# One head ahead of the others: reordering the start of a clustered-attention kernel, and moving copies from VectorE to ScalarE

## The chip, the core and the metric

The kernel runs on one core of a Trainium2 chip. Its time is the device time of one execution in microseconds (us); the time before is the median of three runs. Engines are called as the profile calls them: PE is TensorE's matmul side (PEld its weight loads), DVE VectorE, ACT ScalarE, POOL GpSimd, SP SyncE.

## The reference

Attention over 4 batches, 8 heads, 768 tokens and a head size of 64, in which a query sees a key only if both fall into the same of 16 clusters; then a gated feed-forward layer (512 to 1536 to 512) on its output.

```python
q_assign = np.argmax(np.einsum('bhsd,hcd->bhsc', q_n, c_n), axis=-1)
k_assign = np.argmax(np.einsum('bhsd,hcd->bhsc', k_n, c_n), axis=-1)
mask = q_assign[:, :, :, None] == k_assign[:, :, None, :]
scores = np.where(mask, scale * np.matmul(q, k.transpose(0, 1, 3, 2)), -1e9)
attn = softmax(scores)                       # written out in the reference
x = np.matmul(attn, v)                       # heads side by side: 3072 x 512
xn = x / np.sqrt(np.mean(x * x, -1, keepdims=True) + 1e-06) * rms_g
g = xn @ w_gate
out = (g * sigmoid(g) * (xn @ w_val)) @ w_out
```

## The kernel before

**The mask as extra rows.** The kernel never builds the mask. For each head it keeps q and k transposed in bf16, `qext` and `kext`, 64 rows each, and below them 16 rows with a one in the row of the token's cluster. The score product over 80 rows is then the plain score plus a large constant where the clusters agree, and the exponential with a bias of minus that constant (`off`) leaves nothing of the others.

**Making the operands of a head.** `trans(g, h, part)` (L202) transposes k (part 1) or q (part 0) of head h of group g on PE in three products into a PSUM tile `tq` and copies it to `qkT` in SBUF, on ACT (L214) or, if told so, on DVE (L212). A group is four heads: half a batch. `cast` (L220) writes the bf16 rows from `qkT`; K0, K1, Q0, Q1 in the code are the halves of k and q of a head (even and odd tokens in the first four groups' arrays). Unit 0 needs K0, K1 and Q0 of a head before its scores, Q1 only in unit 1. For batch 0 the cluster rows come from `pair_clusters(p)` (L293): four products of 32 rows (two heads, q and k) into one PSUM tile, then on DVE a transpose in blocks of 32 (L245), the largest of each 16 (L250), and a compare with it (L254) into the tile `pads[p]`; `under(n, m)` (L298) transposes 32 rows of `pads` to below the rows of head n (L300), and `head(n)` does it for k and q.

**Units, gaps, hooks.** Attention is done in eight units: one batch, half of its queries, all eight heads. A unit has 24 gaps, each opened by `scores(u, h, i)` (L306): two products (L316) into one of two PSUM buffers of the pool `ps_s`, and one exponential on ACT of 128 x 768 (L320). In the second gap of a head come the products with v of the head before (`pv`, L324), after every second head the normalization on DVE (L339, L341). What else is issued in a gap of unit 0 is listed by hand in `first` (L605): a number is the gap, a function its work, and `more` (one dummy product that keeps PE busy) stands where there is none. The order of issue is the program's order: on each engine instructions run in the order of the text, and wait there for their operands.

**The prologue** (L519 to L555) makes heads 0 and 1 before the first scores, in this order: k, then q of head 0, k and q of head 1, the cluster steps of both together (`pair_clusters(0)`), the casts on POOL, then k and q of heads 2 and 3 and of head 4 (`tokens(1, 0)`), the second half of k of head 1 cast on ACT, two dummy products, and the rows of heads 0 and 1 by `under`. POOL's casts, conversions of v (`vcast`), the clearing of the other `pads` and the issue of weight loads stand in one line behind one another.

**The start of the feed-forward of unit 0** lies in unit 1. `rms(0)` (L362) computes the norm on DVE after the last `pv` of unit 0; in gap 5 of unit 1 `xtrans_all(0)` (L382) transposes the 128 x 512 blocks of x on PE into two PSUM tiles, `ps[0]` for columns c = 0 and 1 and `ps[1]` for c = 2 and 3, and copies them to `xnT`, scaled by `gcol`: c = 0 to 2 on DVE (L391), c = 3 on ACT (L393). Then each of 12 columns f has a gate product and a value product over the four c (L405). The q and k of group 3 are transposed in unit 1, the q copies by DVE, the k copies by ACT (L455).

Of the kernel before, what the change touches and what calls it, by code (L numbers as in the profile page):

```python
# [9 lines left out]
F32 = mybir.dt.float32  # L10
BF16 = mybir.dt.bfloat16
I32 = mybir.dt.int32
AX = mybir.AxisListType.X
ALU = mybir.AluOpType
# [8 lines left out]
def kernel(  # L23
# [12 lines left out]
    nc = tc.nc  # L36
    B, H, S, D = q.shape
    NC = centroids.shape[1]
    DM = moe_w_gate.shape[0]
    DF = moe_w_gate.shape[1]  # L40
    P = 128
    ST = S // P
    HT = ST // 2
    UQ = HT * P
    HG = 4
# [13 lines left out]
    pool = lambda n, b, **kw: ctx.enter_context(tc.tile_pool(name=n, bufs=b, **kw))  # L59
# [3 lines left out]
    asg = pool("asg", 1)  # L63
    ptp = pool("ptp", 3)
    xp = pool("xp", 1)
    small = pool("small", 3)
    gate = pool("gate", 3)
    outp = pool("outp", 3)
    ps_s = pool("ps_s", 2, space=PSUM)
    ps_a = pool("ps_a", 1, space=PSUM)  # L70
    ps_g = pool("ps_g", 3, space=PSUM)
# [13 lines left out]
    def load_qk(n):  # L85
        if n < B * H:
            load(n, 0)
            load(n, 1)

    def load_v(n, vq=None):  # L90
        if n >= B * H:
            return
        stagedv[n] = stage.tile([P, ST, D], F32, tag="vs", name="vs", bufs=NV)
        (vq or nc.sync).dma_start(out=stagedv[n], in_=src(v, n))
# [55 lines left out]
    for i in range(P // 32):  # L150
        r = slice(32 * i, 32 * i + 32)
# [12 lines left out]
    cblk = const.tile([P, H, 2 * NC], F32)  # L164
# [35 lines left out]
    qkT = {}  # L200

    def trans(g, h, part, on=None):  # L202
        if (g, h // 2) not in qkT:
            qkT[g, h // 2] = qk32.tile([P, 2, 2, UQ], F32, tag="qkT", name="qkT")
        qk = staged[g * HG + h]
        ps = ps_g.tile([P, UQ], F32, tag="gen", name="tq")
        for i in range(HT):
            nc.tensor.transpose(ps[:, i * P:(i + 1) * P], qk[:, part, 2 * i:2 * i + 2].rearrange("p t d -> p (t d)"),  # L208
                                ident_f)
        to, by = qkT[g, h // 2][:, h % 2, part], 1.0 / ZS if part else 1.0  # L210
        if on is nc.vector:
            nc.vector.tensor_scalar_mul(to, ps, by)  # L212
        else:
            nc.scalar.activation(to, ps, ACT.Copy, scale=by)  # L214
# [5 lines left out]
    def cast(on, g, h, part, es=(0, 1)):  # L220
        for e in es:
            to = cols((kext if part else qext)[g % 4][:D, h], g, e)
            of = qkT[g, h // 2][e * D:(e + 1) * D, h % 2, part]
            if on is nc.scalar:
                nc.scalar.copy(to, of)
            else:
                on.tensor_copy(to, of)  # L227

    def vcast(n):
        nc.gpsimd.tensor_copy(vbf[n // HG % 4][:, n % HG, :, :D], stagedv[n])  # L230


    scT = {}

    NB = UQ // 32

    def cluster_products(g, what, ps=None):

        if ps is None:
            ps = ps_g.tile([P, UQ], F32, tag="gen", name="sc")  # L240
        for i, (h, m) in enumerate(what):
            nc.tensor.matmul(ps[32 * i:32 * i + 32], lhsT=cblk[:, g * HG % H + h],  # L242
                             rhs=qkT[g, h // 2][:, h % 2, m], start=True, stop=True)
        sct = asg.tile([P, UQ], F32, tag="scT", name="scT", bufs=2)
        nc.vector.transpose(sct, ps)  # L245
        return sct.rearrange("p (b e c) -> p b e c", e=2, c=NC)

    def largest(cl):
        mx = small.tile([P, NB, 2], F32, tag="mx", name="mx")
        nc.vector.tensor_reduce(mx, cl, axis=AX, op=ALU.max)  # L250
        return mx

    def compare(to, cl, mx):
        nc.vector.tensor_tensor(to, cl, mx.unsqueeze(3).broadcast_to([P, NB, 2, NC]), op=ALU.is_equal)  # L254

    def cluster_steps(g, m):

        of = {}

        def products():  # L260
            of["cl"] = cluster_products(g, [(h, m) for h in range(HG)])

        def most():
            of["mx"] = largest(of["cl"])

        def same():
            of["ohT"] = asg.tile([P, UQ], BF16, tag="ohT", name="ohT", bufs=2)
            compare(of["ohT"].rearrange("p (b e c) -> p b e c", e=2, c=NC), of["cl"], of["mx"])

        def back():  # L270
            put[g, m] = asg.tile([P, UQ], BF16, tag="oh", name="oh", bufs=3)
            nc.vector.transpose(put[g, m], of["ohT"])  # L272

        return [products, most, same, back]
# [3 lines left out]
    def place(on, g, m):  # L278

        ext = (kext if m else qext)[g % 4]  # L280
        for h in range(HG):
# [7 lines left out]
    pads = [(xp if p == 0 else outp).tile([P, NB, 32, 2], BF16, tag="o_sb" if p else "gvT", name=f"pads{p}")  # L289
            for p in range(H // 2)]  # L290
    nc.gpsimd.memset(pads[0][:, :, NC:], 0.0)

    def pair_clusters(p, ps=None):  # L293
        g, h = divmod(2 * p, HG)
        cl = cluster_products(g, [(h, 0), (h + 1, 0), (h, 1), (h + 1, 1)], ps)
        compare(pads[p][:, :, :NC].rearrange("p b c e -> p b e c"), cl, largest(cl))

    def under(n, m):  # L298
        i = 32 * (2 * m + n % 2)
        nc.vector.transpose((kext if m else qext)[n // HG][D:D + 32, n % HG].bitcast(I32),  # L300
                            pads[n // 2][i:i + 32].rearrange("p b c e -> p (b c e)").bitcast(I32))

# [79 lines left out]
    def xtrans_all(u):  # L382

        xnT[u] = xp.tile([P, CC, UQ], BF16, tag="xnT", name="xnT")
        ps = [ps_g.tile([P, 2, UQ], BF16, tag="gen", name="tx") for _ in range(CC // 2)]
        for t in range(HT):
            for c in range(CC):
                nc.tensor.transpose(ps[c // 2][:, c % 2, t * P:(t + 1) * P], xn[u][:, t, c * P:(c + 1) * P], ident)
        for c in range(CC):
            if c < 3:  # L390
                nc.vector.tensor_scalar_mul(xnT[u][:, c], ps[c // 2][:, c % 2], gcol[:, c:c + 1])  # L391
            else:
                nc.scalar.activation(xnT[u][:, c], ps[c // 2][:, c % 2], ACT.Copy, scale=gcol[:, c:c + 1])  # L393
# [56 lines left out]
    def group_work(g):  # L450

        t, c = [], []
        for h in range(HG):
            n = g * HG + h
            t += [(0.3, lambda h=h: trans(g, h, 0, nc.vector if g == 3 else None)), (0.3, lambda h=h: trans(g, h, 1))]  # L455

            def others(n=n):
                vcast(n)
                load_qk(n + NQ)
                load_v(n + NV)  # L460

            def both(h=h, f=others):
                cast(nc.gpsimd, g, h, 0)
                f()
                cast(nc.vector, g, h, 1, (0,))
            if g == 2:
                c.append((0.0, others))
            else:
                c += [(0.0, both), (0.0, lambda h=h: cast(nc.vector, g, h, 1, (1,)))]
        a = []  # L470
        for m in range(2):
            a += [(0.0 if i else 0.7, f) for i, f in enumerate(cluster_steps(g, m))]
            if g <= 3:
                a.append((0.0, lambda m=m: place(nc.sync if g == 2 else nc.gpsimd, g, m)))
        if g > 3:
            a.append((0.0, lambda: [place(nc.gpsimd, g, m) for m in range(2)]))
        return t, c, a
# [25 lines left out]
    def out_work(u):  # L503
        return [(0.86, lambda t=t, p=p: out_mm(u, t, p)) for t in range(UNITS[u][2]) for p in range(3)]
# [6 lines left out]
    def tokens(g, h, on=None):  # L511
        trans(g, h, 1, on)
        trans(g, h, 0, on)

    def casts(on, n, *what):
        for m, e in what:
            cast(on, n // HG, n % HG, m, (e,))

    K0, K1, Q0, Q1 = (1, 0), (1, 1), (0, 0), (0, 1)  # L519
    pool_ = nc.gpsimd  # L520
    trans(0, 0, 1)
    centroids_t()
    trans(0, 0, 0)
    trans(0, 1, 1)
    trans(0, 1, 0)
    pair_clusters(0, ps_s.tile([P, UQ], F32, tag="s", name="sc"))
    casts(pool_, 0, K0, Q0, K1)
    casts(pool_, 1, K0, Q0)
    load_v(0)
    load_v(1)  # L530
    for n in (6, 7):
# [6 lines left out]
    nc.sync.dma_start(out=gcol, in_=moe_rms_g.rearrange("(c p) -> p c", p=P), allow_slow_non_contiguous=True)  # L538
    tokens(0, 2)
    casts(pool_, 2, K0, K1, Q0)  # L540
    tokens(0, 3)
    tokens(1, 0)
    casts(pool_, 3, K0, K1, Q0)
    casts(nc.scalar, 1, K1)
    busy(2)
    for n in (0, 1):
        under(n, 1)
        under(n, 0)
    casts(pool_, 0, Q1)
    casts(pool_, 1, Q1)  # L550
    vcast(0)
# [10 lines left out]
    def second_batch():  # L562
# [2 lines left out]
            load_qk(n)  # L565
        for n in range(H, H + NV):
            load_v(n)

    def head(n):
        under(n, 1)  # L570
        under(n, 0)

    def gap1():
        pair_clusters(1)
# [11 lines left out]
    def gap5():  # L586
# [11 lines left out]
        for n in (6, 7):  # L598
# [3 lines left out]

    early = [lambda h=h, m=m: trans(1, h, m) for h in (2, 3) for m in (1, 0)]
    late = [lambda h=h, m=m: trans(2, h, m, nc.vector if h < 3 else None) for h in range(HG) for m in (1, 0)]
    first = {1: gap1, 2: early[0], 3: early[1], 4: lambda: (early[2](), early[3]()), 5: gap5,  # L605
             7: lambda: head(5), 9: lambda: pair_clusters(3), 10: lambda: head(6),
             13: lambda: (casts(nc.vector, 6, K0, K1), head(7)), 14: lambda: (more(), second_batch())}
    first.update({16: None, 19: None, 22: None})
# [26 lines left out]
    for u in range(1, NU):  # L635
        ffn, o, g = ffn_work(u - 1), out_work(u - 2) if u > 1 else [], u + 2
        if u == 1:
            t, c, a = group_work(2)
            t3, c3, a3 = group_work(3)
            n = LEAD - 4  # L640
# [61 lines left out]
```

The softmax here doesn't subtract the row's maximum and nothing guards it: scores larger than these inputs give would overflow.

## Time and profile before

| | |
|---|---|
| time | 350.19 us (349.99 to 350.3) |
| profiled span | 348.0 us, granted PE clock 1.00 |
| first score product | 11.23 us |
| first exponential | 11.77 us |
| first scores of unit 1 | 33.62 us |
| last `pv` of unit 0 ends | 35.47 us |
| last norm step of x, unit 0 (L369) ends | 40.13 us |
| last of the first four gate products starts | 42.25 us |

The page gives each engine's busy time, then the span in 40 slices of 8.7 us, with the busy share of each engine in tenths. The chain of waits goes back from the last instruction to what released it, over and over; a piece of time on it belongs to the instruction that the end was then waiting for. The timeline lists instructions with start, duration, engine, line, operation, what is written from what with shapes, and in square brackets the idle time before it and who ended it. The start of PE's stretch of L316 to the start of its exponential is the time from scores to ACT.

### The profile page before, as it was taken

What the parts mean: (1) busy time and instruction counts of PE and PEld (TensorE: products, weight loads), DVE (VectorE), ACT (ScalarE), POOL (GpSimd) and SP (SyncE); (2) the same over time, 40 slices, a digit from 0 to 9 for tenths busy, and PEclk for the clock granted to TensorE, in tenths of its full rate; (3) what the DMA queues carried; (4) which work ended last, traced back from release to release, by engine and by line L of the source; (5) the groups of instructions that cost most, each with busy time, mean ns of one, the idle gap of its engine ahead of it and who ended that gap; (6) DMA issues with size and microseconds to landing.
All of it is one profiled execution on the core that took longest, in us unless ns stands there. A gap on an engine that the chain in (4) does not pass through costs nothing.

```text
span 348.0 us, 7965 instructions
## 1 busy us (share of the span) xinstructions
PE 338.3 (97%) x3023; PEld 208.3 (60%) x3040; DVE 220.8 (63%) x540; ACT 258.7 (74%) x446; POOL 111.8 (32%) x224
## 2 busy tenths in 40 slices
PE   8999999999999999999999999999999999999996
PEld 4547656555665557655675657755566656655653
DVE  4889787976568645786267854687456654675430
ACT  5999877766888769887787877978778877764321
POOL 4999595243344403361041801436000000000000
PEclk9999999999999999999999999999999999999999
DMA  7999999072351014501120001000100001001002
GB/s 272 389 189 216 251 207 295 26 249 107 106 179 33 17 60 145 159 18 40 60 93 2 23 33 62 0 6 19 62 32 0 2 33 60 2 1 63 30 2 90
DMA packets 27158, 31.62 MB, mean 91 GB/s; under 512 B 4464, under 2 KB 24176, under 8 KB 27120
## 3 DMA queue, kind: packets, MB, share of 16 engines
q1 hardware_dynamic: 18464, 25.02, 21.4%
q0 software_dynamic: 8368, 5.71, 10.0%
q8 instruction: 24, 0.39, 0.4%
q10 hardware_dynamic: 288, 0.39, 0.3%
q14 instruction: 14, 0.11, 0.1%
HBM read 28.35 MB, written 6.29 MB: 100 GB/s over the span
## 4 chain that ended last, share of the span: by engine, by line
PE 86%; DVE 6%; ACT 5%; issue 1%; DMA 1%; DVEq 0%; ACTq 0%
PE val L405 17%; PE o L430 17%; PE s L316 17%; PE gate L405 16%; PE acc L334 9%; PE tq L208 4%; PE sc L242 4%; ACT pT L320 3%; PE tx L379 1%; ACT qkT L214 1%; DVE x L341 1%; DVE th L414 1%; PE o L441 1%; DMA c_in<-in_centroids_dram 1%; DVE gvT L418 1%
## 5 line engine op out<-in xcount | busy, mean ns | idle before, releaser
L320 ACT ACTIVATE pT<-s,off 128x768 bf16<-128x768 f32 x192 | 170.3, 904 | 36.1 <-PE s L316 35.2
L316 PE MATMUL s<-qext,kext 80*128 80x384 bf16 x384 | 94.4, 327 | 2.1 <-ACT pT L320 1.2
L405 PE MATMUL gate<-xnT,wg 128*128 128x384 bf16 x384 | 78.7, 326 | 0.8 <-DVE gvT L418 0.4
L405 PE MATMUL val<-xnT,wv 128*128 128x384 bf16 x384 | 78.2, 326 | 1.1 <-DVE th L414 1.1
L414 DVE SCALAR_TENSOR_TENSOR th<-th,gate 128x384 f32<-128x384 f32 x84 | 46.4, 552 | 50.2 <-ACT th L413 50.0
L430 PE MATMUL o<-wo,gvT 128*128 128x512 bf16 x259 | 66.0, 379 | 0.9
L227 POOL CAST qext<-qkT 64x384 bf16<-64x384 f32 x64 | 35.0, 552 | 79.3 <-ACT qkT L214 34.1
L316 PEld LDWEIGHTS <-kext 80*128 80x128 bf16 x384 | 36.4, 98 | 32.5 <-issue 7.6
L405 PEld LDWEIGHTS <-wv 128*128 128x128 bf16 x384 | 36.1, 97 | 27.0 <-issue 5.4
L413 ACT ACTIVATE th<-gate 128x384 f32<-128x384 f32 x84 | 41.1, 489 | 14.7 <-PE gate L405 14.3
L418 DVE SCALAR_TENSOR_TENSOR gvT<-th,val 128x384 bf16<-128x384 f32 x84 | 46.2, 550 | 7.9 <-PE val L405 3.3
L405 PEld LDWEIGHTS <-wg 128*128 128x128 bf16 x384 | 35.8, 97 | 25.3 <-issue 4.1
L334 PEld LDWEIGHTS <-pT 128*128 128x128 bf16 x1152 | 43.4, 97 | 9.3 <-DVE x L341 0.9
L334 PE MATMUL acc<-vbf,pT 128*128 128x65 bf16 x1152 | 45.5, 193 | 0.2 <-DVE x L341 0.2
L430 PEld LDWEIGHTS <-gvT 128*128 128x128 bf16 x276 | 25.8, 97 | 25.1
L208 PE MATMUL tq<-ident_f,qk 128*128 128x128 f32 x192 | 30.2, 277 | 0.3 <-ACT qkT L214 0.3
L380 DVE TENSOR_SCALAR xnT<-tx,gcol 128x384 bf16<-128x384 bf16 x28 | 10.6, 413 | 28.7 <-PE tx L379 28.7
L283 POOL DMA_DIRECT2D qext<-oh x40 | 19.1, 487 | 29.1 <-DVE oh L272 24.2
L214 ACT ACTIVATE qkT<-tq 128x384 f32<-128x384 f32 x54 | 25.0, 497 | 3.4 <-PE tq L208 3.0
L208 PEld LDWEIGHTS tq<-ident_f,qk 128*128 128x128 f32 x192 | 23.5, 142 | 6.6 <-issue 0.8
L433 ACT COPY o_sb<-o 128x512 f32<-128x512 f32 x23 | 13.5, 585 | 17.4 <-PE o L430 17.4
L283 POOL DMA_DIRECT2D kext<-oh x40 | 19.1, 485 | 9.6 <-DVE oh L272 9.6
(79 smaller groups left out, 249.7 us busy)
## 6 DMA issues: line engine op xcount, KB each, us to landing
qk<-in_q_dram SPq DMA_DIRECT2D x32, 192.0 KB, 3.8
vs<-in_v_dram SPq DMA_DIRECT2D x32, 192.0 KB, 4.3
out_dram<-o_sb SPq DMA_DIRECT2D x23, 256.0 KB, 2.0
qk<-in_k_dram SPq DMA_DIRECT2D x30, 192.0 KB, 3.9
wg<-in_moe_w_gate_dram POOLq DMA_DIRECT2D x4, 384.0 KB, 8.1
wv<-in_moe_w_val_dram POOLq DMA_DIRECT2D x4, 384.0 KB, 10.2
wo<-in_moe_w_out_dram POOLq DMA_DIRECT2D x3, 512.0 KB, 7.0
qext<-oh POOLq DMA_DIRECT2D x40, 12.0 KB, 1.6
```

Of the source, the lines that this page charges most:

```text
L208: nc.tensor.transpose(ps[:, i * P:(i + 1) * P], qk[:, part, 2 * i:2 * i + 2].rearrange("p t d -> p (t d)"), ident_f)
L214: nc.scalar.activation(to, ps, ACT.Copy, scale=by)
L227: on.tensor_copy(to, of)
L283: on.dma_start(out=ext[D:D + NC, h, e * UQ:(e + 1) * UQ], in_=put[g, m][32 * h + e * NC:32 * h + (e + 1) * NC])
L316: nc.tensor.matmul(ps[:, j, :w] if nt == HT else flat[:, j * w:(j + 1) * w], lhsT=cols(kext[g % 4][:KR, hh], g, kc // HT, kc % HT * P, (kc ...
L320: nc.scalar.activation(pT[u, h][:, n * i:n * i + n, :w], of, ACT.Exp, bias=off, scale=scale * ZS)
L334: nc.tensor.matmul(acc[:, h % 2, t], lhsT=pT[u, h][:, kc, t * P:(t + 1) * P], rhs=vbf[g % 4][:, hh, kc % HT * 2 + kc // HT], start=kc == 0 ...
L405: nc.tensor.matmul(ps, lhsT=w[:, c, f * P:(f + 1) * P], rhs=xnT[u][:, c, :n], start=c == 0, stop=c == CC - 1)
L413: nc.scalar.activation(th, ps, ACT.Tanh, scale=0.5)
L414: nc.vector.scalar_tensor_tensor(th, th, 1.0, ps, op0=ALU.add, op1=ALU.mult)
L418: nc.vector.scalar_tensor_tensor(gvT[u][:, f, :n], gates[u], 0.5, ps, op0=ALU.mult, op1=ALU.mult)
L430: nc.tensor.matmul(outs[u], lhsT=gvT[u][:, f, t * P:(t + 1) * P], rhs=wo[:, f], start=f == 0, stop=f == FC - 1)
```

## The change

It does three things. Head 0's cluster steps no longer wait for head 1: `pair_clusters` takes a list of heads, and the places of the 32-row blocks in `pads[0]` are renumbered by `slot`, so that the two blocks of one head lie side by side and can be worked on alone (64 partitions). Head 1's own steps, and its rows, follow behind head 0's rows; the first copy of all (k of head 0) is made by DVE, head 4's transposes go from the prologue to gap 0 of the first unit, in place of a dummy product, and K1 of head 1 is cast by POOL instead of ACT. Second, the copies of transposed x are split by PSUM tile: c = 0 and 1 on DVE, c = 2 and 3 on ACT. Third, all copies of group 3 are made on ACT. The first is for an earlier first exponential, the second so that the two engines don't share a PSUM bank, the third to take work from DVE.

```diff
+    def slot(n, m):
+        return 32 * (2 * (n % 2) + m if n < 2 else 2 * m + n % 2)
+
-    def pair_clusters(p, ps=None):
+    def pair_clusters(p, heads=(0, 1)):
         g, h = divmod(2 * p, HG)
-        cl = cluster_products(g, [(h, 0), (h + 1, 0), (h, 1), (h + 1, 1)], ps)
-        compare(pads[p][:, :, :NC].rearrange("p b c e -> p b e c"), cl, largest(cl))
+        what = [(h + i, m) for i in heads for m in range(2)]
+        at = [slot(2 * p + i, m) for i in heads for m in range(2)]
+        r = slice(min(at), max(at) + 32)
...
+        nc.vector.transpose(sct[r], ps[r])
...
+        nc.vector.tensor_reduce(mx, cl, axis=AX, op=ALU.max)
+        nc.vector.tensor_tensor(pads[p][r, :, :NC].rearrange("p b c e -> p b e c"), cl,
+                                mx.unsqueeze(3).broadcast_to([mx.shape[0], NB, 2, NC]), op=ALU.is_equal)
...
-            if c < 3:
+            if c < 2:
                 nc.vector.tensor_scalar_mul(xnT[u][:, c], ps[c // 2][:, c % 2], gcol[:, c:c + 1])
...
-            t += [(0.3, lambda h=h: trans(g, h, 0, nc.vector if g == 3 else None)), (0.3, lambda h=h: trans(g, h, 1))]
+            t += [(0.3, lambda h=h: trans(g, h, 0)), (0.3, lambda h=h: trans(g, h, 1))]
...
-    trans(0, 0, 1)
+    trans(0, 0, 1, nc.vector)
     centroids_t()
     trans(0, 0, 0)
     trans(0, 1, 1)
+    pair_clusters(0, (0,))
+    casts(pool_, 0, K0, Q0, K1)
+    head(0)
     trans(0, 1, 0)
-    pair_clusters(0, ps_s.tile([P, UQ], F32, tag="s", name="sc"))
-    casts(pool_, 0, K0, Q0, K1)
-    casts(pool_, 1, K0, Q0)
+    casts(pool_, 1, K0, Q0, K1)
...
     casts(pool_, 2, K0, K1, Q0)
+    pair_clusters(0, (1,))
+    head(1)
     tokens(0, 3)
-    tokens(1, 0)
     casts(pool_, 3, K0, K1, Q0)
-    casts(nc.scalar, 1, K1)
     busy(2)
-    for n in (0, 1):
-        under(n, 1)
-        under(n, 0)
...
-    first = {1: gap1, 2: early[0], 3: early[1], 4: lambda: (early[2](), early[3]()), 5: gap5,
+    first = {0: lambda: tokens(1, 0), 1: gap1, 2: early[0], 3: early[1], 4: lambda: (early[2](), early[3]()), 5: gap5,
```

More of the change, by code (lines that the diff above doesn't have):

```diff
@@ L235, with cluster_products @@
     NB = UQ // 32
-    def cluster_products(g, what, ps=None):
-        if ps is None:
-            ps = ps_g.tile([P, UQ], F32, tag="gen", name="sc")
+    def cluster_products(g, what):
+        ps = ps_g.tile([P, UQ], F32, tag="gen", name="sc")
         for i, (h, m) in enumerate(what):
@@ L291 @@
     nc.gpsimd.memset(pads[0][:, :, NC:], 0.0)
-    def pair_clusters(p, ps=None):
+    def slot(n, m):
+        return 32 * (2 * (n % 2) + m if n < 2 else 2 * m + n % 2)
+    def pair_clusters(p, heads=(0, 1)):
         g, h = divmod(2 * p, HG)
-        cl = cluster_products(g, [(h, 0), (h + 1, 0), (h, 1), (h + 1, 1)], ps)
-        compare(pads[p][:, :, :NC].rearrange("p b c e -> p b e c"), cl, largest(cl))
+        what = [(h + i, m) for i in heads for m in range(2)]
+        at = [slot(2 * p + i, m) for i in heads for m in range(2)]
+        r = slice(min(at), max(at) + 32)
+        pool = ps_g if p else ps_s
+        ps = pool.tile([P, UQ], F32, tag="gen" if p else "s", name="sc")
+        for a, (hh, m) in sorted(zip(at, what)):
+            nc.tensor.matmul(ps[a:a + 32], lhsT=cblk[:, g * HG + hh], rhs=qkT[g, hh // 2][:, hh % 2, m],
+                             start=True, stop=True)
+        sct = asg.tile([P, UQ], F32, tag="scT", name="scT", bufs=2)
+        nc.vector.transpose(sct[r], ps[r])
+        cl = sct[r].rearrange("p (b e c) -> p b e c", e=2, c=NC)
+        mx = small.tile([P, NB, 2], F32, tag="mx", name="mx")[r]
+        nc.vector.tensor_reduce(mx, cl, axis=AX, op=ALU.max)
+        nc.vector.tensor_tensor(pads[p][r, :, :NC].rearrange("p b c e -> p b e c"), cl,
+                                mx.unsqueeze(3).broadcast_to([mx.shape[0], NB, 2, NC]), op=ALU.is_equal)
     def under(n, m):
-        i = 32 * (2 * m + n % 2)
+        i = slot(n, m)
         nc.vector.transpose((kext if m else qext)[n // HG][D:D + 32, n % HG].bitcast(I32),
@@ L513, in tokens, with head @@
         trans(g, h, 0, on)
+    def head(n):
+        under(n, 1)
+        under(n, 0)
     def casts(on, n, *what):
@@ L567, in second_batch @@
             load_v(n)
-    def head(n):
-        under(n, 1)
-        under(n, 0)
     def gap1():
```

## The prediction

> **What bounds the kernel now.** I read the page's first two parts, then the chain of waits for the first 60 us, then the timeline of each engine between 4 and 64 us. The page says where not to look:
>
> ```profile
> PE 338.3 (97%) x3023; PEld 208.3 (60%) x3040; DVE 220.8 (63%) x540; ACT 258.7 (74%) x446; POOL 111.8 (32%) x224
> POOL 4999595243344403361041801436000000000000
> ```
>
> From 65 us on the chain is TensorE work almost alone and the edit moves nothing there, so only shifts that reach 65 us count. GpSimd's 32% is a mean over a kernel whose last third it leaves empty: it is full in slices 2 to 4, up to 35 us, the first unit of attention. The chain, cut to the two places that the edit touches (start, duration, what):
>
> ```profile
> 5.33 0.39 ACT qkT L214
> 5.76 0.55 PE tq L208 x3
> 6.30 1.47 PE sc L242 x8
> 7.80 0.59 DVE scT L245
> ...
> 10.52 0.58 DVE qext L300
> 11.23 0.50 PE s L316 x2
> ...
> 40.13 0.47 DVE qkT L212
> 40.60 0.99 DVE xnT L391 x3
> 41.62 0.59 ACT xnT L393
> 42.25 0.32 PE gate L405
> ```
>
> First: the first score waits for eight passes of cluster products of two heads, then five VectorE steps; the passes themselves wait in the middle for head 1's q (the 0.55 us of transposes). Second: a copy of q of group 3 and three copies of transposed x stand one behind the other on VectorE, then ScalarE makes the fourth copy, then the first gate product ends.
>
> The timeline shows a third thing that the chain does not, GpSimd. It casts without a gap from 5.77 to 26 us, in an order written by hand:
>
> ```profile
> 19.43 0.50 POOL L230 CAST vbf<-vs 128x384 bf16<-128x384 f32 x1
> 19.44 0.94 DVE L254 TENSOR_TENSOR pads<-scT,mx 128x384 bf16<-128x384 f32 x1
> 19.88 0.94 POOL L227 CAST kext<-qkT 64x384 bf16<-64x384 f32 x1
> 24.88 0.58 DVE L254 TENSOR_TENSOR pads<-scT,mx 128x384 bf16<-128x384 f32 x1
> 24.91 1.00 POOL L227 CAST qext<-qkT 64x384 bf16<-64x384 f32 x1
> 26.21 0.13 PEld L316 LDWEIGHTS <-kext 80*128 80x128 bf16 x2 [0.49 <-POOL qext L227]
> ```
>
> The cast at 24.91 is q of head 5. It ends at 25.91; head 5's first scores start at 26.24, as soon as the exponential two before them (25.20 to about 26.1) has left their PSUM buffer. So GpSimd is only some 0.2 to 0.3 us from setting that start. Both kinds of instruction stretch when they meet: a compare takes 0.58 us alone and 0.94 us here, a cast 0.61 alone and 0.94 to 1.00 here.
>
> **What the Trainium skill says.** "SBUF — State Buffer", Who interferes with whom: a VectorE instruction with two SBUF inputs and a GpSimd instruction that reads SBUF exclude each other, and the later one waits; a GpSimd instruction that only writes does not take part. The trace agrees: the lines above, and the compare at 14.35, which meets a memset, takes 0.59 us. "PSUM — Partial Sum Buffer", PSUM bank collisions raise a hardware error: two engines must not be in one bank and quadrant together. This agrees with the fourth x copy, which shares a bank with the third: it starts at 41.62, after VectorE's third, although ScalarE had been idle for 1.37 us. "ScalarE: Activation LUTs", What ACT_TABLE_LOAD costs: a per-partition scale adds some 93 ns to an activation. The trace: 0.58 us for the x copy against 0.49 us for L214, with a constant scale.
>
> **Part 1, the first copy on VectorE and head 0 alone.** k's transposes end at 4.67; ScalarE's table load and first exponential hold its copy back to 5.33. VectorE is free at 4.46, so its copy (0.47 to 0.55 us, L212's row) runs 4.72 to 5.27, and the two centroid copies (0.29 each) end at 5.78 instead of 5.54. Head 0's products, half of the 0.85 us that eight passes take undisturbed at 12.23, run 5.85 to 6.30. VectorE's first step starts at 6.35 instead of 7.80: 1.45 us earlier. The chain from there to the first exponential (7.80 to 11.77, 3.97 us) keeps its steps, since half the partitions leave the 384 elements of each lane. That the reduction in partitions saves nothing is taken from L300: 32 partitions, 384 elements, 0.57 us, as L245 with 128. First exponential: 10.32.
>
> **Part 2, what ScalarE gives back.** Two copies of k and q of head 4 move from ahead of the first exponential (where ScalarE now idles more) to behind it: two steps of 0.37 us, 0.75 together. The cast of 0.62 us that ScalarE loses stood in front of an idle stretch of 0.47, so it returns nothing by itself. ScalarE is nearly full from 11.77 to 35, so 1.45 - 0.75 = 0.70 us of lead remain, 0.8 with the small gaps between its second and third exponential closed.
>
> **Part 3, what VectorE gives back.** Pair 0 is now done in halves: one more transpose, reduction and compare, 0.58 + 0.55 + 0.6 to 0.8, with gaps 1.95 us. Starting 1.45 earlier, head 1's rows end near 12.85 against 12.27. That is still before pair 1's products are wanted (13.15), so pair 1 starts some 0.25 us earlier. PE waits for none of it: head 1's first scores are at 14.40 now.
>
> **Part 4, GpSimd, where I expect the lead to go.** It starts at 5.33 instead of 5.77: 0.44 earlier. It takes over the cast of head 1's K1: one step of the run of casts, 0.65 us. And VectorE makes five compares instead of four before 24.9, at moments when GpSimd casts. Before, three met: 0.17 + 0.33 + 0.39 = 0.89 us over casts of 0.61 (0.78, 0.94, 1.00). After, four or five should meet, some 0.3 us each: 1.2 to 1.5. Sum: 0.65 - 0.44 + (0.3 to 0.6) = 0.5 to 0.8 us later, middle 0.65. The bounds: 0.2 if no further one meets, 1.0 if all five cost 0.36. Three things queue behind it:
> - The memset of pads 1 (14.45 to 14.86) must precede head 2's rows, which start at 15.05, right after their compare. They would start at 15.5, and of VectorE's lead 0.2 us stays at pair 2.
> - q of head 5 ends at 25.91 + 0.65 = 26.56; scores from 26.66 instead of 26.24, 0.42 later. From that, 0.17 comes back, since the 0.17 us for which ScalarE idles before 28.70 go back to VectorE's normalization (L341), which would now be done earlier.
> - v of head 5 (29.09 to 29.60) ends at 30.25; its product starts at 29.99 now.
>
> All three say that the lead of 0.7 us is turned into a loss of some 0.25 us by 35 us.
>
> **Part 5, copies of x by bank.** VectorE's chain of the norm from 35.5 is untouched. In it the q copy (0.47) goes away, and the third x copy (0.33). ScalarE gets that q copy: one exponential (37.36) and what follows it are 0.37 later, so the scores at 38.43 start at 38.7, the four dummy products follow, and the transposes of x (now to 40.59) end near 40.72. ScalarE then makes the copies of its own bank without waiting for VectorE: 40.77, a step of 0.47, and 0.58, to 41.82 instead of 42.20. Gain 0.38 us; 0.55 if the transposes are not delayed, 0.1 if ScalarE comes free later.
>
> **Part 6, the other three q copies of group 3,** 55.63, 59.15 and 62.97 on VectorE. PE's waits near there (0.66 us at 55.77, 0.44 at 63.10) end with th, ahead of the copy on VectorE, so taking it away frees nothing that is waited for. On ScalarE a copy of 0.37 fits into idle stretches of 1.19 and 0.70 us ahead of the exponentials at 56.96 and 64.35; the one near 59.7 delays two exponentials into 0.30 us of idle. Zero, with 0.1 either way.
>
> **Sum:** -0.25 + 0.38 = 0.13 us gained: 350.19 - 0.13 = **350.1 us**, not to be told from no change.
>
> **Rivals.**
> - *The lead survives* (0.30). GpSimd's meetings with compares fall on memsets or between casts, and head 5 is not late. For it: the first compare can move off a cast by a shift of 0.2 us, and the margin at head 5 exists. Against: GpSimd has no gap before 26 us. It keeps 0.7 to 0.8 us, plus 0.38: 350.19 - 1.15 = 349.0.
> - *GpSimd is later and ScalarE becomes the bound at the norm* (0.20). A delay of 1.0 instead of 0.65 moves head 5's v to 30.6, 0.6 past its use, and this is not made good, as ScalarE is full there (eight exponentials back to back take 6.45 us from 28.70 on). If ScalarE's extra copy also delays the x copies, 0.1 is left of part 5. 350.19 + 0.6 + 0.3 (the compares stretched on VectorE's own chain) - 0.1 = 351.0, slower.
>
> **How the numbers follow.** The forecast has 0.50. The range reaches to both rivals: 349.0 to 351.0. A change of 0.2% is 0.7 us. Faster by that: the survivor's cases but for those where less than 0.3 us of lead is left (0.27), and a low GpSimd delay of the forecast (0.08), together 0.35. Slower: most of the second rival (0.15) and the forecast's upper end (0.05), 0.20. Within: 0.45.
>
> **What would show it.** First exponential near 10.3 (part 1); the third compare, of pair 1, at about 14 (part 3); GpSimd's cast of q of head 5 ending after 26.3, and a wait of LDWEIGHTS on it longer than 0.49 (part 4); both ScalarE x copies starting before VectorE's second ends, the first gate group's last product starting 1.75 us after the last norm step instead of 2.12, 40.13 to 42.25 (part 5). If that cast ends before 25.9 and the last pv of the first unit ends before 35.0 instead of 35.47, part 4 was wrong and the time is near 349.

## The result, and the profile after

The changed kernel takes 348.94 us (348.61 to 349.06, four runs) against 350.14 us for the kernel before: ratio 0.9964, 95% interval 0.9947 to 0.9981. Run again beside other kernels it took 349.28 us (348.49 to 350.03, nine runs) against 350.07: 0.9974, 0.9960 to 0.9987. So it is about 1 us faster; the prediction had 350.1 us and a range from 349.0.

The page of the changed kernel shows as little as the one before did: 98% of PE, and GpSimd full in the same slices.

```profile
PE 338.4 (98%) x3039; PEld 208.2 (60%) x3039; DVE 221.4 (64%) x539; ACT 259.9 (75%) x449; POOL 111.9 (32%) x225
POOL 5999595244335304271042801535000000000000
```

What tells more is the difference of the two traces place by place. The 192 exponentials come in the same order in both kernels, so each can be compared with itself. The profiled runs differ by 1.15 us; the table says by when they do (us, positive: the changed kernel is earlier; the numbers in the table's head are times in us). The other rows belong to the experiments below.

| kernel | first exp. | end of unit 0 (35) | after first gate (45) | 58 | 64 | 69 | end |
|---|---|---|---|---|---|---|---|
| changed | 1.02 | 0.30 | 0.65 | 0.62 | 1.11 | 1.11 | 1.15 |
| after2 (the same again) | 1.01 | 0.29 | 0.65 | 0.60 | 1.08 | 1.08 | 1.13 |
| a_start2 | 1.02 | 0.32 | 0.32 | 0.33 | 0.33 | 0.33 | 0.33 |
| a_split | -0.05 | -0.07 | 0.46 | 0.21 | 0.22 | 0.15 | 0.18 |
| a_q3 | 0.00 | -0.04 | -0.21 | -0.12 | 0.36 | -0.02 | 0.19 |
| a_q3p | 0.00 | -0.01 | -0.18 | -0.18 | 0.31 | 0.31 | 0.35 |
| d_four | 0.93 | 0.26 | 0.61 | 0.59 | 1.07 | 1.07 | 1.11 |
| c_dve8 | 1.02 | 0.32 | 0.67 | 0.64 | 0.65 | 0.56 | 0.61 |
| c_dve7 | 1.01 | 0.28 | 0.80 | 0.59 | 1.08 | 0.21 | 0.24 |
| f_memset | 1.02 | 0.52 | 0.87 | 0.80 | 1.29 | 1.29 | 1.33 |
| h_place | 1.02 | 0.31 | 0.67 | 0.63 | 1.11 | 1.11 | 1.15 |
| f_place | 1.02 | 0.53 | 0.88 | 0.85 | 1.34 | 1.33 | 1.37 |

One correction is in the table. The first cluster product starts at 5.69 to 6.44 us in the nine profiles with the new start, and at 6.23 to 6.90 in the four with the old one. That offset, against 5.89 of the changed kernel and 6.23 of the kernel before, is taken out of every row. These two starts are 0.34 us apart, the medians of the nine and of the four 0.32, so the two traces are a fair pair, though four are few. In the two profiles of the changed kernel the scatter comes from PE: the transposes of k start at 3.96 in both, but of the six transposes right ahead of the cluster products each takes 0.27 us in one, while in the other the first four take 0.42 and the fifth 0.34; they end at 5.59 and 6.11. Why PE is slower for a while is not shown; the granted clock reads 1.00 in both. The scatter is as large as what is looked for, so single times and even medians of five runs say less here than one trace does.

Four places make up the 1.15: 1.02 at the first exponential shrinks to 0.30 by the end of unit 0; the x copies add 0.36; between 58 and 64 us another 0.49 come; the last 0.04 lie near 71 us. Here are the lines for each. First the start, in the timelines of PE, of VectorE and of ScalarE of the changed kernel:

```profile
5.89 0.84 PE L304 MATMUL sc<-qkT,cblk 128*32 128x384 f32 x4 [0.30 <-POOL kext L227]
...
7.79 0.84 PE L304 MATMUL sc<-qkT,cblk 128*32 128x384 f32 x4
```

```profile
6.77 0.57 DVE L307 STREAM_TRANSPOSE scT<-sc 64x384 f32<-64x384 f32 x1 [1.08 <-PE sc L304]
7.38 0.55 DVE L310 TENSOR_REDUCE mx<-scT 64x24 f32<-64x384 f32 x1
7.96 0.84 DVE L311 TENSOR_TENSOR pads<-scT,mx 64x384 bf16<-64x384 f32 x1
```

```profile
10.76 0.90 ACT L336 ACTIVATE pT<-s,off 128x768 bf16<-128x768 f32 x1 [0.74 <-PE s L332]
```

Head 0's two products take 0.84 us, not half of the four's 0.85, and its first VectorE step starts at 6.77, not 6.35; the first exponential is at 10.76. Next, the chain of waits of the changed kernel up to head 5 (start, duration, what):

```profile
23.93 0.63 POOL kext L227
24.55 0.06 issue
24.61 0.79 POOL kext L227
25.40 0.06 issue
25.46 0.61 POOL qext L227
26.07 0.04 issue
26.12 0.52 PE s L332 x2
```

From 5.26 us to here the chain lies on POOL alone: GpSimd bounds unit 0 up to head 5. Its cast of q of head 5 ends at 26.06, 0.15 later than before. Then the copies of x in ScalarE's timeline and in VectorE's:

```profile
38.58 1.76 ACT L336 ACTIVATE pT<-s,off 128x768 bf16<-128x768 f32 x2
40.50 1.05 ACT L409 ACTIVATE xnT<-tx,gcol 128x384 bf16<-128x384 bf16 x2 [0.16 <-PE tx L404]
```

```profile
40.39 0.74 DVE L407 TENSOR_SCALAR xnT<-tx,gcol 128x384 bf16<-128x384 bf16 x2 [0.55 <-PE tx L404]
```

Both of ScalarE's copies run from 40.50 without waiting for VectorE, whose two run from 40.39 to 41.13. Last, PE's timeline at 62 us, of the kernel before and then of the changed kernel:

```profile
62.17 0.49 PE L208 MATMUL tq<-ident_f,qk 128*128 128x128 f32 x3
63.10 0.81 PE L405 MATMUL val<-xnT,wv 128*128 128x384 bf16 x4 [0.44 <-DVE th L414]
```

```profile
61.54 0.49 PE L208 MATMUL tq<-ident_f,qk 128*128 128x128 f32 x3
61.99 0.81 PE L421 MATMUL val<-xnT,wv 128*128 128x384 bf16 x4
```

The 0.44 us for which this value product waited for VectorE's th are gone. This is the largest single gain that reaches the end, and the prediction had put it at zero.

### The profile page after: what moved, and what is told of

It is laid out like the page before. It is cut to its first block, busy times and chain, and to the rows that moved or that the text cites. A ratio compares the mean times of both kernels' runs of the same rounds, so it can differ in the third digit from the quotient of the medians.

```text
span 346.8 us, 7983 instructions
## 1 busy us (share of the span) xinstructions
PE 338.4 (98%) x3039; PEld 208.2 (60%) x3039; DVE 221.4 (64%) x539; ACT 259.9 (75%) x449; POOL 111.9 (32%) x225
## 4 chain that ended last, share of the span: by engine, by line
PE 83%; ACT 6%; POOL 6%; DVE 3%; issue 1%; POOLq 0%; ACTq 0%; DVEq 0%
PE o L446 17%; PE val L421 17%; PE gate L421 17%; PE s L332 15%; PE acc L350 8%; ACT pT L336 4%; PE tq L208 3%; PE sc L241 3%; POOL kext L227 2%; POOL qext L227 2%; PE tx L395 1%; PE warm L117 1%; PE o L457 1%; DVE th L430 1%; POOL vbf L230 1%
## 5 line engine op out<-in xcount | busy, mean ns | idle before, releaser
L446 PE MATMUL o<-wo,gvT 128*128 128x512 bf16 x276 | 67.4, 379 | 0.0
L214 ACT ACTIVATE qkT<-tq 128x384 f32<-128x384 f32 x57 | 26.6, 496 | 3.5 <-PE tq L208 3.2
```

Source lines behind the costliest of these rows:

```text
L446: nc.tensor.matmul(outs[u], lhsT=gvT[u][:, f, t * P:(t + 1) * P], rhs=wo[:, f], start=f == 0, stop=f == FC - 1)
```

## The experiments

**Each part by itself.** The first kernel has the new start alone, the second the x copies by bank alone, the third group 3's copies on ScalarE alone. a_start2 is the kernel of a_start again: the times below are of a_start, the row of the table is of a_start2.

```diff
 a_start and a_start2: the kernel before, with all of the change but
-            if c < 2:
+            if c < 3:
-            t += [(0.3, lambda h=h: trans(g, h, 0)), ...
+            t += [(0.3, lambda h=h: trans(g, h, 0, nc.vector if g == 3 else None)), ...
 a_split: the kernel before, with
-            if c < 3:
+            if c < 2:
 a_q3: the kernel before, with
-            t += [(0.3, lambda h=h: trans(g, h, 0, nc.vector if g == 3 else None)), ...
+            t += [(0.3, lambda h=h: trans(g, h, 0)), ...
```

> The kernel before with the new start alone (head 0 ahead, head 1 behind it, head 4's transposes in gap 0, K1 of head 1 on GpSimd); the copies of x and of group 3 stay as before. Theory (three gains in three places, that add): only the 0.30 us that the last exponentials of unit 0 show is won, about 349.85 us against 350.15; PE's wait for th at 63 us stays at 0.44 us, and the last of the first gate products comes 0.3 us earlier than before. Rival S (the earlier start carries the whole, the later gains are its echoes): 349.0 us. Rival P (the forecast: GpSimd takes more than the lead): 350.4 us.

> The kernel before with the new order of the start alone (head 0 through its cluster steps first, K1 of head 1 on GpSimd); x copies and group 3's copies as before. Theory (the changed kernel's trace read by stages): the first exponential 1.0 us earlier than in the kernel before, 0.1 to 0.3 us of it left at the exponentials of head 5 and at the end of unit 0, because q of head 5 then waits for GpSimd's casts; nothing gained at the x copies and at 62 us, so 0.3 us at the end. Rival (the lead survives unit 0 and what it brings is larger than the stages show): 0.5 us or more at the end. Second rival (a lead of the start is taken by the wait for VectorE's th at 63 us, whose time is set by VectorE): 0 at the end.

> The kernel before with the copies of x split by PSUM bank alone (c = 0, 1 on VectorE, c = 2, 3 on ScalarE). Theory: unit 0 ends as before; the q copy of group 3 still stands ahead of the x copies on VectorE, ScalarE starts its two at about 40.65 and the last of the first gate products starts at 41.75 instead of 42.25: 0.5 us, 349.65 us. The wait for th at 63 us stays. Rival (the gain near 42 us came from the q copy's leaving VectorE, not from the banks): 350.1 us.

> The kernel before with all copies of group 3 on ScalarE alone; x copies three and one as before. Theory: near 42 us it wins 0.1 us or so (VectorE starts the x copies earlier, but the transposes of x come later, and ScalarE's copy still waits for VectorE's third); near 63 us it wins 0.45 to 0.5, because the value product there is given the PSUM buffer that the q copy on ScalarE sets free, and not that of the gate product, whose reader th is late. 349.55 us. Rival P (the forecast: the copies taken off VectorE free nothing that is waited for): 350.05 us, the wait for th at 63 us stays.

By medians: a_start 349.83 us (ratio 0.9991, 0.9982 to 1.0000), a_split 350.21 (1.0001, 0.9991 to 1.0012), a_q3 350.1 (0.9993, 0.9984 to 1.0002). Added up, that is a third of what the change brings as a whole, and none can be told from nothing with confidence. The 349.65 and 349.55 us expected of the last two were missed; their traces end 0.18 and 0.19 us ahead, which the intervals allow. The rows of the table explain the rest.

The start is worth 0.33 us and keeps it to the end: the later waits don't swallow it. Its parts (head 0 alone, the first copy on VectorE, the moved casts and transposes) were not tried apart. The x copies win 0.53 at 45 us by themselves, and the q copy that moves to ScalarE takes 0.17 of that back (a_q3 at 45 us); together that is the 0.36 of the changed kernel. It is the split that frees ScalarE, not the q copy: in a_q3, with the q copy off VectorE and x still three and one, ScalarE's copy waits for VectorE's third as before, while ScalarE's two in a_split wait for PE's transposes alone. ScalarE's timeline of a_q3:

```profile
41.88 0.58 ACT L393 ACTIVATE xnT<-tx,gcol 128x384 bf16<-128x384 bf16 x1 [1.15 <-DVE xnT L391]
```

a_split then loses 0.25 at 54 to 57 us, where two casts meet a third. VectorE's timeline of the kernel before, then of a_split:

```profile
54.42 0.70 DVE L227 CAST kext<-qkT 64x384 bf16<-64x384 f32 x2
```

```profile
54.61 0.98 DVE L227 CAST kext<-qkT 64x384 bf16<-64x384 f32 x2
55.62 0.55 DVE L414 SCALAR_TENSOR_TENSOR th<-th,gate 128x384 f32<-128x384 f32 x1
```

The two casts took 0.70 in the kernel before; here they meet GpSimd's cast of v (54.50 to 55.01), th is later by as much, and the value product behind it waits 0.94 us instead of 0.66. With group 3's copies off VectorE this loss does not appear (0.65 to 0.62 in the changed kernel), and with three of them back it does (0.80 to 0.59 in c_dve7, below); how the copies bring the meeting about was not followed. And a_q3 has the whole 0.48 at 58 to 64 us, without the other two parts, but loses 0.38 at 67 us, of which below. Start 0.33, x copies 0.53 - 0.17, and 0.48 make 1.17, against 1.15 measured.

**Is the price of the cluster products their number?** In d_four two more products stand beside each head's two; they go to rows that nothing reads.

```diff
+        if p == 0:
+            for a, (hh, m) in sorted(zip(at, what)):
+                a = (a + 64) % P
+                nc.tensor.matmul(ps[a:a + 32], lhsT=cblk[:, g * HG + hh], rhs=qkT[g, hh // 2][:, hh % 2, m],
+                                 start=True, stop=True)
```

> The changed kernel with two more products beside the two of head 0's half of pair 0, and of head 1's half (into rows of the same PSUM tile that nothing reads). The prediction took two products as half the price of four. Theory (products into different groups of 32 PSUM rows start together and run side by side, so the price is that of one pass): four products still take 0.84 us in the first cluster step, within 0.05 us, VectorE's first step of the clusters stays at 6.77 us and the first exponential at 10.76 us, all counted from the same start, and the total does not move. Rival (the price grows with the number of products, as the prediction had it): the four take about 1.7 us, and the first exponential comes some 0.8 us later, at 11.6 us.

Its PE timeline, L304 the kernel's own products and L309 the added ones, each in two passes:

```profile
6.44 0.59 PE L304 MATMUL sc<-qkT,cblk 128*32 128x384 f32 x2
6.45 0.58 PE L309 MATMUL sc<-qkT,cblk 128*32 128x384 f32 x2
6.85 0.50 PE L304 MATMUL sc<-qkT,cblk 128*32 128x384 f32 x2
6.87 0.49 PE L309 MATMUL sc<-qkT,cblk 128*32 128x384 f32 x2
```

The added ones start 0.01 to 0.02 us behind the others and run beside them. From 6.44 to the last end, 7.36, are 0.92 us, and 0.85 for the second head's (8.42 to 9.27), against 0.84 for two: twice the products, at most 0.08 us more, not the 0.8 that a price per product would add. The first exponential is 0.09 us later than the changed kernel's, the end 0.04; as PE's transposes right ahead still took 0.42 us each in this run, even that cannot safely be put down to the added products. That products run side by side stands in the Trainium skill, "TensorE: Matmul & The Clock Gate", Packing small matmuls: products whose outputs start at different multiples of 32 PSUM partitions lie in different column groups of the array and run concurrently. The trace agrees, with starts 0.01 to 0.02 us apart; the prediction did not use it.

**What bounds unit 0?** In f_memset the clearing of three pads, 1.12 us of GpSimd at 14.96, moves into the 3.28 us for which GpSimd waits for the first copy.

```diff
-    nc.gpsimd.memset(pads[0][:, :, NC:], 0.0)
+    for p in range(H // 2):
+        nc.gpsimd.memset(pads[p][:, :, NC:], 0.0)
...
-    for p in range(1, H // 2):
-        nc.gpsimd.memset(pads[p][:, :, NC:], 0.0)
```

> The changed kernel with the three clearings of the later pads moved from the middle of GpSimd's run of casts (1.08 us near 15) to its first instructions, where it idles for 3.3 us. Theory (after the change GpSimd's queue is what bounds unit 0 up to head 5's scores): its cast of q of head 5 ends near 25.0 instead of 26.06, head 5's scores no longer wait for it, ScalarE's idle 0.39 us before 26.72 goes away, and the time falls by 0.3 to 0.6 us: 348.3 to 348.65. Rival (ScalarE or VectorE bound unit 0 as much, GpSimd's place on the chain is a tie): 348.85 to 348.95, as the changed kernel.

Of the lead 0.52 instead of 0.30 us is left at the end of unit 0, and 1.33 instead of 1.15 at the end. The chain of waits of f_memset shows who took over, here around 23 us:

```profile
21.97 0.90 ACT pT L337
22.89 0.91 ACT pT L337
23.80 0.04 issue
23.84 0.50 PE s L333 x2
24.34 0.55 PE acc L351 x18
24.89 0.34 PE s L333 x2
```

No piece of POOL is left on it between 5 and 28 us: ScalarE and PE are the bound, and the lead they leave, 0.52, is near the 0.57 that the changed kernel still had ahead of head 5. So GpSimd was the bound in the changed kernel, as the prediction said, but cost 0.2 us, less than the 0.3 to 0.6 that were expected here. (The 0.37 us named in the expectation of f_place below is the plain difference of two profiled runs; 0.20 of it is f_memset's earlier start.) The median of f_memset, 349.1 us (0.9970, 0.9960 to 0.9980), did not show its gain; the last experiments say why that can happen.

**What changed at 62 us: VectorE's load, or the buffer?** gate, value and transpose products share three PSUM buffers. In the kernel before, the value product at 62 us gets the buffer of a gate product, which VectorE's th sets free. With the q copies on ScalarE, the same product gets the buffer of a q transpose, which ScalarE's copy has already freed. If that is the cause, it matters which copy moves, not how many. So one kernel puts only head 3's copy back on VectorE, and another all but head 3's.

```diff
 c_dve8: the changed kernel, with
+            ... trans(g, h, 0, nc.vector if g == 3 and h in (3,) else None)
 c_dve7: the changed kernel, with
+            ... trans(g, h, 0, nc.vector if g == 3 and h in (0, 1, 2) else None)
```

> The changed kernel with one of group 3's four copies of transposed q (that of head 3) back on VectorE. Theory (hand-over of PSUM buffers: the value product at 62 us takes the buffer of the product planned to be released before it; with this copy on VectorE that is again the gate's, which VectorE releases late): that value product waits for VectorE's th step again, 0.44 us as in the kernel before, and of the gain of 1.15 us about 0.65 is left at the end. Rival (what counts is the time that four copies take from VectorE, 0.34 us each): one copy of four costs a quarter of 0.48, that is 0.12 us, and about 1.03 us is left.

> The changed kernel with three of group 3's four copies of transposed q (those of heads 0, 1 and 2) back on VectorE and head 3's on ScalarE. Theory (hand-over of PSUM buffers): the value product at 62 us takes a buffer that ScalarE releases, as in the changed kernel, and does not wait for VectorE's th; the 0.44 us stay won though three copies are back. Head 0's copy stands among the copies of x and may cost up to 0.3 us there, so 0.8 to 1.15 us of the gain are left at the end. Rival (time taken from VectorE): three quarters of 0.48, 0.36 us, are lost at 62 us, on top of what head 0's copy costs.

PE's timeline of c_dve8, then of c_dve7:

```profile
62.28 0.81 PE L421 MATMUL val<-xnT,wv 128*128 128x384 bf16 x4 [0.44 <-DVE th L430]
```

```profile
62.05 0.81 PE L421 MATMUL val<-xnT,wv 128*128 128x384 bf16 x4
```

One copy back on VectorE brings the 0.44 us back whole; three copies back bring none of it, and PE stays 1.08 ahead at 64 us. By medians c_dve8 takes 349.75 us (0.9986, 0.9980 to 0.9993) and c_dve7 349.03 (0.9968, 0.9957 to 0.9980): 0.7 us apart in the same runs, the one with less work on VectorE the slower. The traces also record on which semaphore, that is on whose counter of finished instructions, this product waits: on VectorE's in the kernel before and in c_dve8, on ScalarE's in the changed kernel, a_q3 and c_dve7. And VectorE is not late anywhere: its th starts 0.99 to 1.00 us after the first product of the q transpose in all five. The hand-over of the buffer is the cause, the load is not.

**What takes 0.87 us at 67 us?** The profiled run of c_dve7, the slowest of its seven (348.61 to 349.58), falls back behind 64 us, from 1.08 to 0.21. Its chain of waits there, and SyncE's queue in its timeline:

```profile
65.97 0.65 PE val L421 x4
66.62 0.71 issue
67.33 0.65 PE s L332 x3
```

```profile
58.64 0.33 SPq L94 DMA_DIRECT2D vs<-in_v_dram  x1
59.60 5.81 SPq L282 DMA_DIRECT2D qext<-oh  x8
65.51 3.06 SPq L282 DMA_DIRECT2D kext<-oh  x5
```

"issue" is a wait for nothing that the profile names. The product at 67.33 is the first that reads group 2's arrays. It needs cluster rows that SyncE writes in sixteen small transfers, all of q's ahead of k's, and behind the last load of v; head 0's two of k leave at 65.51 and 66.09. The first of the two lands at 67.24, 0.09 us before the product starts. The same 0.09 us stand between landing and start in a_q3 (67.51 and 67.60), c_dve8 (66.70 and 66.79) and a_split (67.95 and 68.04), the other rows that fall between 64 and 69 us by more than the odd 0.01. In the changed kernel the two left at 63.81 and 64.99, and the first landed at 66.14, 0.27 us before its product; in after2 0.12 us were left. So this would be the next bound, and it moves from run to run: each transfer follows the one before by 0.63 us, but one in each run by 0.7 to 1.7, for a reason not shown. Three kernels with those transfers in another order, head by head, test this, beside the changed kernel again:

```diff
-                a.append((0.0, lambda m=m: place(nc.sync if g == 2 else nc.gpsimd, g, m)))
+                a.append((0.0, lambda m=m: place(nc.gpsimd, g, m) if g != 2 else by_head() if m else None))
...
+    def by_head():
+        for h in range(HG):
+            for m in range(2):
+                for e in range(2):
+                    nc.sync.dma_start(out=(kext if m else qext)[2][D:D + NC, h, e * UQ:(e + 1) * UQ],
+                                      in_=put[2, m][32 * h + e * NC:32 * h + (e + 1) * NC])
```

h_place is the changed kernel with this, f_place f_memset with this, a_q3p a_q3 with this.

> The changed kernel once more, on the chip and beside the runs of before that the three kernels sent with it share: 348.9 us, 1.1 to 1.2 us under before. Theory (the next bound behind the gain is a transfer: the score product of the first head of group 2, at 66.9 us, needs the cluster rows that SyncE's queue writes, and in the changed kernel's trace they landed just then): some runs wait there for up to 0.9 us and the spread of the runs reaches up to 349.8 us. Rival (nothing waits there): the runs lie as close as those of before, within 0.9 us, and none of it comes from 67 us.

> The changed kernel with the sixteen small transfers that write group 2's cluster rows issued head by head (two of q, two of k, then the next head) in place of all eight of q ahead of all eight of k; they take 0.63 us each on SyncE's queue, so head 0's four are issued 2.5 us after the first and not 6.3 us. Theory (landing of these rows is the next bound, met by some runs only): the median falls by 0.1 to 0.4 us against the changed kernel, no run loses time at 67 us, and what the trace shows as won up to 64 us stays won to the end. Rival (the landing never binds, or another wait stands right behind it): same as the changed kernel within 0.1 us.

> The changed kernel with the three memsets of the pads moved into GpSimd's idle time at the start of the program (as in f_memset, whose trace won 0.37 us more than the changed kernel's but whose median, 349.1 us, did not show it) and with group 2's rows issued head by head. Theory (GpSimd bounds unit 0 in the changed kernel, and the landing at 67 us takes the gain back in some runs): 348.5 us, 0.4 us under the changed kernel in the same runs and 1.6 us under before. Rival (the 0.37 us of the trace is chance): 348.9 us, no better than the changed kernel.

> The kernel before with group 3's copies of transposed q on ScalarE (as in a_q3, which gained only 0.05 us by its median, though its trace kept 0.48 us at 62 us and then waited 0.22 to 0.38 us at 67 us) and with group 2's rows issued head by head. Theory (the hand-over of buffers at 62 us is worth 0.48 us, ScalarE's later exponentials cost 0.2 us of it, and a late landing at 67 us took the rest in a_q3): 0.3 us under before, 349.85 us, and no wait at 67 us in the trace. Rival (the copies on ScalarE are worth nothing by themselves): as a_q3, 350.1 us.

| | us, median (range, runs) | ratio to before, 95% |
|---|---|---|
| after2 | 349.28 (348.49 to 350.03, 9) | 0.9974, 0.9960 to 0.9987 |
| h_place | 349.10 (348.75 to 349.16, 5) | 0.9966, 0.9954 to 0.9978 |
| f_place | 348.55 (348.35 to 348.96, 5) | 0.9956, 0.9944 to 0.9968 |
| a_q3p | 349.75 (349.44 to 350.09, 16) | 0.9990, 0.9982 to 0.9997 |

The clearest is a_q3p: its trace keeps at 69 us what it had at 64 (0.31), where a_q3 fell from 0.36 to -0.02, and its median is 0.35 us lower than a_q3's; beside their own runs of before the medians are 0.32 and 0.05 us lower, and the two intervals overlap widely, so here the trace decides. In f_place SyncE's queue begins nearly as late as in c_dve7, but head 0's k rows leave 5 us earlier:

```profile
58.06 0.33 SPq L94 DMA_DIRECT2D vs<-in_v_dram  x1
59.30 1.20 SPq L471 DMA_DIRECT2D qext<-oh  x2
60.58 1.17 SPq L471 DMA_DIRECT2D kext<-oh  x2
```

and PE, 1.3 us ahead of before, does not wait at 66.8. h_place ends as the changed kernel by its trace, as expected where nothing waits in that run. Its median fell by 0.18 us, within the expected 0.1 to 0.4, but its interval overlaps after2's. That its five runs reach no higher than 349.16 while after2's reach 350.03 fits the landing, and also fits the chance of nine runs against five; that the changed kernel itself waits there in some runs is not shown. f_place is the fastest version by its median: 1.5 us under before, and 0.7 under after2 in the same runs, though the two intervals overlap slightly.

## Why the prediction was wrong

The total was out by 1.0 us: 0.13 forecast, 1.15 by the traces. Two terms carry it, the lead of the start (-0.25 forecast, 0.30 measured) and part 6 (0 forecast, 0.49 measured).

- **Part 1, first term mis-sized.** "Half of the 0.85 us that eight passes take": two products took 0.84 us, because products in different groups of 32 rows run side by side (d_four). That alone moves the first exponential from 10.32 to 10.74; it was at 10.76. The other steps of the part held within 0.1 us.
- **Part 2 right.** Of the lead 0.65 us went between the first exponential and the one at 18 us (1.02 to 0.37), where 0.75 was forecast.
- **Part 3 right in the conclusion, not in the time.** The third compare was to come at about 14 us and came at 14.59: 0.42 from part 1, the rest from two compares of 0.84 and 0.85. Pair 1 therefore started 0.23 us later (13.38 against 13.15), not 0.25 earlier; the part's own terms gave 12.77 for the end of head 1's rows, not 12.85. No exponential waited for it.
- **Part 4, mechanism right, size wrong.** GpSimd became the bound and q of head 5 came later, but its cast ended at 26.06 and not at 26.56. The term that failed is the meetings with compares: forecast 1.2 to 1.5 us for four or five, measured 0.17, 0.19, 0.17 and 0.18 (casts of 0.78, 0.80, 0.67 and 0.79 against 0.61, and 0.50 for v), 0.71, less than the 0.89 of the three before. The rest fell on the compares, 0.84, 0.85 and 0.87 against 0.58, as it had before on two of three (0.80 and 0.94); what decides the share was not tested. The delay of 0.15 is then the cast taken over (0.67) less the earlier start (0.51) and the cheaper meetings (0.18), plus 0.17 by which the steps of the first five casts grew. (The part's upper bound is 1.1 by its own terms, not 1.0.) The 0.17 us that were to come back at 28.70 did come back (0.13 at head 5, 0.30 at the end of unit 0).
- **Part 5 right.** 0.36 measured, 0.38 forecast.
- **Part 6 failed.** "PE's waits near there (...) end with th, ahead of the copy on VectorE, so taking it away frees nothing that is waited for." The first half is right: the wait ended with th. But who a product waits for is decided by which buffer it is given, and moving the copies changed that. c_dve8 and c_dve7 show it: 0.44 us hang on the one copy of head 3.
- **Not in the prediction: the landing at 67 us.** It took the chain from 65 us on for TensorE work that the edit does not move. In the trace of the kernel before, head 0's first k rows land at 67.29, 0.23 us before their product at 67.52, so a gain could be lost there; in c_dve7 0.87 us were.

Of the rivals, "the lead survives" had the time, 349.0, but not for its reason: it kept 0.7 to 0.8 us of lead, where 0.30 was left; the rest was part 6. Nothing of the other rival happened: ScalarE's extra q copies cost 0.17 us, not the norm.

## What to carry to other kernels

A wait on a PSUM buffer belongs to the pairing of producer and buffer, not to the engine that it names: before putting a moved copy at nothing, ask which buffer each product behind it will be given afterwards, and who frees that one. A time for "n products" from the profile may be divided only after looking at their starts; those that run side by side can cost the same for two as for four (0.84 and 0.85 us here). And where the parts of a change are smaller than the scatter of its start, compare instruction by instruction from a common event, and then look for the next bound right behind the gain, here a queue of small transfers with no time to spare.

## What the runs showed of the hardware that was not expected

Small products into different groups of 32 PSUM rows start 0.01 to 0.02 us apart; four take 0.85 to 0.92 us, two 0.84. A compare and a cast that meet cost the cast 0.17 to 0.19 us in the changed kernel, against 0.17, 0.33 and 0.39 in the kernel before, at other offsets. The same program's first cluster product started 0.39 us later in one run than in another (5.89 and 6.28 us in the two profiles of the changed kernel), because PE's transposes ahead of it took up to 0.42 us each and not 0.27. And a product that waits for the landing of a small transfer starts 0.09 us after it (four traces).
